# Six heads without the shift, and the first weights in quarters for four heads at once

**Chip, cores, metric.** One core of a Trainium2 chip. The metric is the device time of one execution in microseconds (us), lower is better. Executions of one kernel spread over some 5 us (0.4%).

## The reference, cut to what matters

```python
mod = silu(c) @ w_mod                      # six rows of 1024: sa, ca, ga, sb, cb, gb
h = layernorm(x) * (1 + ca) + sa           # x: 2048 x 1024
q = h @ wq                                 # 32 heads of 128
o = softmax(q k^T / sqrt(128)) v           # 4 kv heads, the last 512 keys
x = x + ga * (o @ wo)
x = x + gb * ffn(layernorm(x) * (1 + cb) + sb)
```

The change touches only the first 55 us or so. There the kernel must get x (1 MB of the first 512-row chunk), the scale columns `ca` of w_mod (2 MB), the first query weights (1 MB), the shift columns `sa` (2 MB) and keys and values from HBM before the attention can run.

## The kernel before

A helper tracks buffers and puts semaphore waits before each operation; so nearly all matmuls have the line L272. The query of a head is `(n * (1+ca) + sa) @ wq`, n the normed x. The shift `sa` comes late. So the first heads ("without the shift", NQ0 = 8) are projected from `n * (1+ca)` and kept in f32; later one column `sa @ wq` per head (16 one-column matmuls for two heads) is added: `q_bias_mm`, `q_shifted`. Other heads are projected inside the attention rounds, from shifted hT.

```python
for hf in range(2):                 # loads, in order of issue
    load_wca(hf)                    # half of the scale columns: 4 loads of 256 KB, rows of 512 columns
    load_wq0(hf)                    # half of the contraction of heads 0 to 3, 512 KB
load_wq(1)                          # heads 4 to 7, 1 MB
load_k(0)
for k2 in range(DT // 2):
    load_wsa(k2)                    # shift columns, 4 x 512 KB
load_v(0); load_wq(2); load_x(1)
# ... [cut] norm, transposes, first half of the scales; then the opening:
for kc in range(HK):
    for h in range(3):              # three heads on the first 256 rows, later on the other 256
        q_first(h, kc, 0, 2 * P)
# ... [cut] second half, head 3; then:
qproj_mm(4, ...); q_raw(4); mod_sa(0); k_turn(0, BB)     # mod_sa(k2): shift columns of load k2
qproj_mm(5, ...); q_raw(5); mod_sa(1)
qproj_mm(6, ..., 0, HK); mod_sa(2); qproj_mm(6, ..., HK, DT); q_raw(6); mod_sa(3)
qproj_mm(7, ..., 0, HK); q_bias_mm(0, 2, BB); q_shifted(0)
qproj_mm(7, ..., HK, DT); q_raw(7); q_shifted(1)
# attention, round i: scores(i-1), exp on ScalarE, pv(i-2); and in pre0(i):
if i in (1, 3, 5): q_bias_mm(i + 1, i + 3, QB)
if i < NQ0 + 1:
    if i % 2 == 0: qproj(NQ0 - 1 + i // 2)   # a projection in every second round
elif i + 3 < NDI: qproj(i + 3)
```

(`mod_sa(k2)` is 16 one-column matmuls, two rows of tiles by eight columns.)

The softmax here doesn't subtract the row's maximum and nothing guards it: scores larger than these inputs give would overflow.

## Time and profile before

| | before |
|---|---|
| median of the first 3 runs, then of 6 | 1162.29, 1159.84 us |
| lowest, highest of the 6 | 1158.30, 1163.55 us |
| span of the profiled execution | 1156.8 us, clock 1.000 |
| TensorE busy | 1145.8 us, 99% |

The prediction below shows the lines. One more view, the waits between 29.5 and 60 us (who waited for whom: us in total, times, longest), shows what the loop part of the change is after: in the first rounds TensorE's weight loads wait for exps on ScalarE, since only every second round has a projection to do.

```profile
PEld ps L272 <- ACT arena L796: 2.4, 3, 1.0
```

### The profile page before, as it was taken

How to read it: one execution, taken by the hardware profiler on the slowest of the kernel's cores; microseconds unless marked ns; L12 is line 12 of the kernel's file. 1: busy time of each engine (PE TensorE's matmuls, PEld its weight loads, DVE VectorE, ACT ScalarE, POOL GpSimd, SP SyncE). 2: the span in 40 equal slices, each digit the busy share in tenths (PEclk: the TensorE clock that was granted, in tenths of full speed). 3: DMA queues.
4: the chain of work that ended last, by engine and by line, in shares of the span. 5: the costliest groups of instructions: out<-in, count | busy, mean ns of one | idle time of the engine just before them, and what ended most of it. 6: DMA issues, size and time to landing. Idle time of an engine off the chain costs nothing.

```text
span 1156.8 us, 18111 instructions
## 1 busy us (share of the span) xinstructions
PE 1145.8 (99%) x7029; PEld 585.5 (51%) x7029; DVE 825.1 (71%) x1651; ACT 532.0 (46%) x745; POOL 67.6 (6%) x137
## 2 busy tenths in 40 slices
PE   8999999999999999999999999999999999999999
PEld 5555656654446566656444444444444444444444
DVE  4777997747667777786657898777558777776536
ACT  3867787720127777787100354454110444444110
POOL 1100231000000111111000010000000000000000
DMA  9789899986808898945764332423874423234443
GB/s 321 135 178 216 214 211 207 239 188 180 238 16 186 205 209 212 205 96 126 195 198 151 94 88 73 110 74 100 209 206 140 119 76 107 73 98 131 131 159 109
DMA packets 298532, 179.96 MB, mean 156 GB/s; under 512 B 140496, under 2 KB 287696, under 8 KB 298448
## 3 DMA queue, kind: packets, MB, share of 16 engines
q1 hardware_dynamic: 235472, 92.31, 37.3%
q10 hardware_dynamic: 54336, 55.05, 15.2%
q0 software_dynamic: 8640, 31.46, 8.6%
q8 instruction: 55, 0.90, 0.3%
q14 instruction: 29, 0.24, 0.1%
HBM read 125.96 MB, written 19.92 MB: 126 GB/s over the span
## 4 chain that ended last, share of the span: by engine, by line
PE 93%; DMA 2%; DVE 2%; issue 1%; ACT 1%; SPq 1%; DVEq 0%; ACTq 0%
PE ps L272 93%; DMA arena<-in_A_wq_dram 1%; DMA arena<-nsc 1%; DVE arena L826 1%; ACT arena L796 1%; DMA arena<-arena 1%; DVE arena L897 0%; SPq L341 0%; DVE arena L1053 0%; DVE st L417 0%; SPq L310 0%; SPq L359 0%; DVE arena L843 0%; DVE nsc L431 0%; DVE arena L1552 0%
## 5 line engine op out<-in xcount | busy, mean ns | idle before, releaser
L272 PE MATMUL ps<-arena 128*128 128x512 f16 (+2 forms) x6800 | 1140.4, 330 | 7.9 <-POOL arena L410 2.2
L272 PEld LDWEIGHTS ps<-arena 128*128 128x128 bf16 (+1 forms) x6800 | 577.8, 98 | 564.5 <-DVE arena L826 7.0
L796 ACT ACTIVATE arena<-ps 128x1024 bf16<-128x1024 f32 x256 | 261.2, 1021 | 43.7 <-PE ps L272 31.9
L829 ACT ACTIVATE tmp<-ps 128x512 f32<-128x512 f32 x167 | 99.7, 597 | 295.5 <-PE ps L272 284.6
L897 DVE TENSOR_TENSOR arena<-arena 128x512 f16<-128x512 bf16 x328 | 133.1, 418 | 3.0
L826 DVE TENSOR_TENSOR arena<-ps,tmp 128x512 bf16<-128x512 f32 (+1 forms) x134 | 91.7, 685 | 50.7 <-PE ps L272 37.8
L829 ACT ACTIVATE nsc<-ps 128x512 f32<-128x512 f32 x84 | 50.1, 596 | 93.2 <-PE ps L272 90.9
L818 DVE TENSOR_TENSOR arena<-ps,rl 128x512 f16<-128x512 f32 x128 | 88.5, 691 | 5.1 <-DVE rl L815 0.7
L826 DVE TENSOR_TENSOR arena<-ps,nsc 128x512 f16<-128x512 f32 x84 | 57.3, 686 | 41.0 <-PE ps L272 29.7
L815 DVE RECIPROCAL rl<-ps 128x4 f32<-128x4 f32 x128 | 23.0, 180 | 75.6 <-PE ps L272 74.8
L1113 DVE TENSOR_TENSOR tmp<-ps,tmp 128x512 f32<-128x512 f32 x32 | 22.0, 689 | 61.0 <-ACT tmp L829 51.4
L1537 ACT ACTIVATE arena<-arena 128x512 f16<-128x512 f16 x84 | 49.9, 624 | 32.7 <-DVE arena L826 32.7
L1037 DVE TENSOR_TENSOR arena<-arena 128x2048 f16<-128x2048 f16 (+3 forms) x56 | 56.0, 1010 | 9.3 <-PE ps L272 8.8
L829 ACT ACTIVATE arena<-ps 128x512 f32<-128x512 f32 x16 | 9.6, 597 | 90.7 <-PE ps L272 90.7
L947 DVE TENSOR_TENSOR arena<-arena 128x512 f16<-128x512 bf16 x120 | 47.8, 419 | 1.4 <-DMA arena<-in_A_wo_dram 0.4
L417 DVE BATCH_NORM_STATS2 st<-x_res 128x6 f32<-128x512 bf16 x58 | 39.5, 682 | 3.7 <-DMA x_res<-in_A_x_dram 3.4
L594 DVE SCALAR_TENSOR_TENSOR arena<-arena 128x1024 bf16<-128x1024 bf16 x32 | 38.9, 1215 | 0.0
L1552 DVE TENSOR_TENSOR arena<-arena 128x512 f16<-128x512 f16 x84 | 35.0, 416 | 0.3
L1114 DVE TENSOR_TENSOR tmp<-tmp,rowb 128x512 f32<-128x512 f32 (+1 forms) x49 | 33.6, 686 | 1.7
L431 DVE TENSOR_SCALAR nsc<-x_res,mv,rstd 128x1024 f16<-128x1024 bf16 (+1 forms) x30 | 16.2, 538 | 22.3 <-DMA arena<-nsc 21.0
L1115 DVE TENSOR_TENSOR arena<-tmp,x_res 128x512 bf16<-128x512 f32 (+1 forms) x33 | 22.3, 676 | 1.1
L826 DVE TENSOR_TENSOR arena<-ps,rowb 128x512 f16<-128x512 f32 x28 | 19.3, 689 | 3.9 <-ACT rowb L829 3.4
(85 smaller groups left out, 325.6 us busy)
## 6 DMA issues: line engine op xcount, KB each, us to landing
arena<-in_A_wq_dram SPq DMA_DIRECT2D x28, 512.0 KB, 5.1
arena<-wo_sum ACTq DMA_DIRECT2D x7, 2048.0 KB, 8.8
arena<-in_B_w_gate_dram SPq DMA_DIRECT2D x28, 512.0 KB, 4.0
arena<-in_B_w_up_dram SPq DMA_DIRECT2D x28, 512.0 KB, 5.1
arena<-wd_sum ACTq DMA_DIRECT2D x8, 1792.0 KB, 7.8
arena<-in_B_w_down_dram ACTq DMA_DIRECT2D x6, 1792.0 KB, 7.2
arena<-in_A_wo_dram POOLq DMA_DIRECT2D x16, 512.0 KB, 4.9
wo_sum<-arena POOLq DMA_DIRECT2D x16, 512.0 KB, 5.0
```

The lines of the kernel that those rows point to most:

```text
L272: T.op(PE, lambda: TE.matmul(out_ap, lhsT, rhs, start=start, stop=stop, skip_group_check=skip), reads=reads, writes=[bank_buf])
L417: T.op(DVE, lambda: V.bn_stats(st_[sl][:, hf * 6:hf * 6 + 6], x_res[:, t, hf * 512:hf * 512 + 512]), reads=[B_x[t]], writes=[B_st[sl]])
L594: T.op(DVE, lambda: V.scalar_tensor_tensor(mt[n % 2], mt[n % 2], 1.0, sc_row, op0=ALU.mult, op1=ALU.mult, accum_out=mcol[:, n:n + 1]), rea ...
L796: T.op(ACT, lambda: A.activation(ex_s[es][:, 2 * kp:2 * kp + 2, :], banks2(SCB + 2 * kp), AF.Exp, scale=att_scale), writes=[PB[SCB + 2 * k ...
L818: T.op(DVE, lambda: V.tensor_tensor(o_s[os_].rearrange("p (a b) d -> p a b d", a=2), psap(PVB * 512, [[512, 2], [130, 2], [1, P]]), rlb, A ...
L826: T.op(DVE, lambda: V.tensor_tensor(out, bank(ba), other, ADD), reads=[ob2], writes=[PB[ba], ob])
L829: T.op(ACT, lambda: A.activation(dst, bank(bk), AF.Copy), writes=[PB[bk], db])
L897: T.op(st, lambda: eng.tensor_tensor(o, a, b, op), reads=rd, writes=[wr])
L947: T.op(DVE, lambda: V.tensor_tensor(o, a, b, SUB), reads=rd, writes=[wr])
L1037: T.op(DVE, lambda: V.tensor_tensor(o, a, b, SUB), reads=rd, writes=[sb])
L1537: T.op(ACT, lambda: A.activation(o, s_, AF.Silu), reads=[sb], writes=[ob])
L1552: T.op(DVE, lambda: V.tensor_tensor(gu[blk][:, p, :], o, s_, MULT), reads=[sb, ob], writes=[B_gu[blk][p]])
```

## The change

The intent: start the first query matmuls sooner, by asking for a quarter of the scales and weights instead of half; have four heads go at once; reach the first scores sooner by projecting only six heads without the shift; give each of rounds 2 to 7 one projection, so that they are even. The order of the later loads follows: half of the second query weights before the shift columns, the other half after. Core of the diff:

```diff
-NQ0 = 8
+NQ0 = 6
-# load_wca(hf): 4 loads of 2 row blocks x 512 columns
+# load_wca(q): 8 row blocks x 256 columns, 1 load (2 for q == 0)
-for hf in range(2):
-    load_wca(hf); load_wq0(hf)
-load_wq(1); load_k(0)
-for k2 in range(DT // 2): load_wsa(k2)
-load_v(0); load_wq(2); load_x(1)
+for q in range(NQR):
+    load_wca(q); load_wq0(q)
+load_wq1(0); load_wsa(0); load_wsa(1); load_k(0); load_wsa(2); load_wsa(3)
+load_v(0); load_wq1(1); load_x(1); load_wq(2)
@@ opening [cut]
+q_four(0, 0, 2 * P)                     # 2 contraction tiles x 4 heads
+mod_ca(1); x_gain(1); x_mod(1, 0, B_hT[0])
+x_first(2, range(HK)); x_first(tl, range(HK)); x_mod(0, 2, B_h0b)
+q_four(1, 0, 2 * P); ...
+mod_ca(3); x_gain(3); x_mod(3, 0, B_hT[0]); q_four(2, 0, CH); q_four(3, 0, CH)
@@ after head 4
-qproj_mm(5), mod_sa(1), half of 6, mod_sa(2), rest of 6, mod_sa(3), half of 7, q_bias_mm, rest of 7
+mod_sa(1), half of 5, mod_sa(2), mod_sa(3), a quarter of 5, q_bias_mm, the last quarter of 5
@@ pre0(i)
-if i in (1, 3, 5): q_bias_mm(i + 1, i + 3, QB)
+if i in (1, 3): q_bias_mm(i + 1, i + 3, XB)
-if i % 2 == 0: qproj(NQ0 - 1 + i // 2)
+if 2 <= i < 8: qproj(i + 4)
```

Also in the change and not shown: three warm-up matmuls fewer (matmuls on zeros, which keep TensorE busy before its data is there), tiles 2 and 3 of x normed whole instead of in halves, other places for the transposes in PSUM, and the norms of the second chunk one round later.

More of the change, by code (lines that the diff above doesn't have):

```diff
@@ L331, in _, with load_wca @@
             HK = DT // 2
-            NQ0 = 8
+            NQ0 = 6
             ND = 12
-            B_wca = [[_Buf("wca%d_%d" % (hf, i)) for i in range(4)] for hf in range(2)]
+            NQR = DT // 2
+            B_wca = [[_Buf("wca%d_%d" % (q, i)) for i in range(2)] for q in range(NQR)]
             B_wsa = [_Buf("wsa%d" % k) for k in range(DT)]
-            wca = [arena.at(OFF_OT[2] + hf * 8 * KB, [DT, 512], BF16, B_wca[hf]) for hf in range(2)]
+            wca = [arena.at(OFF_OT[2] + q * 4 * KB, [DT, 2 * P], BF16, B_wca[q]) for q in range(NQR)]
             wsa = arena.at(OFF_OT[3], [DT, D], BF16, B_wsa)
-            def load_wca(hf):
-                for i in range(4):
-                    T.op(dq("q_wca%d_%d" % (hf, i)), lambda: SP.dma_start(
-                        wca[hf][:, 2 * i:2 * i + 2, :],
-                        w_mod[2 * i * P:(2 * i + 2) * P, D + hf * 512:D + (hf + 1) * 512].rearrange("(k p) n -> p k n", p=P)),
-                         writes=[B_wca[hf][i]])
+            def load_wca(q):
+                parts = 2 if q == 0 else 1
+                m = DT // parts
+                for i in range(parts):
+                    T.op(dq("q_wca%d_%d" % (q, i)), lambda: SP.dma_start(
+                        wca[q][:, i * m:(i + 1) * m, :],
+                        w_mod[i * m * P:(i + 1) * m * P, D + q * 2 * P:D + (q + 1) * 2 * P].rearrange("(k p) n -> p k n", p=P)),
+                         writes=[B_wca[q][i]] if parts == 2 else B_wca[q])
             NWQ = 2
@@ L356, in load_wq, with load_wq0 @@
                     wq_s[gidx], A_wq[:, gidx * 512:(gidx + 1) * 512].rearrange("(k p) n -> p k n", p=P)), writes=B_wq[gidx])
-            def load_wq0(kh):
-                T.op(dq("q_wq0%d" % kh), lambda: SP.dma_start(
-                    wq_s[0][:, kh * HK:(kh + 1) * HK, :],
-                    A_wq[kh * HK * P:(kh + 1) * HK * P, 0:512].rearrange("(k p) n -> p k n", p=P)), writes=[B_wq[0][kh]])
+            B_wq0 = [_Buf("wq0_%d" % q) for q in range(NQR)]
+            def load_wq0(q):
+                T.op(dq("q_wq0%d" % q), lambda: SP.dma_start(
+                    wq_s[0][:, 2 * q:2 * q + 2, :],
+                    A_wq[2 * q * P:(2 * q + 2) * P, 0:512].rearrange("(k p) n -> p k n", p=P)), writes=[B_wq0[q]])
             def load_wsa(k2):
@@ L395, in load_v, with load_wq1 @@
                      writes=[B_vg[gk]])
-            for hf in range(2):
-                load_wca(hf)
-                load_wq0(hf)
-            load_wq(1)
+            B_wq1 = [_Buf("wq1_%d" % m) for m in range(2)]
+            def load_wq1(m):
+                T.op(dq("q_wq1%d" % m), lambda: SP.dma_start(
+                    wq_s[1][:, :, m * 2 * P:(m + 1) * 2 * P],
+                    A_wq[:, 512 + m * 2 * P:512 + (m + 1) * 2 * P].rearrange("(k p) n -> p k n", p=P)), writes=[B_wq1[m]])
+            for q in range(NQR):
+                load_wca(q)
+                load_wq0(q)
+            load_wq1(0)
+            load_wsa(0)
+            load_wsa(1)
             load_k(0)
-            for k2 in range(DT // 2):
-                load_wsa(k2)
+            load_wsa(2)
+            load_wsa(3)
             load_v(0)
+            load_wq1(1)
+            load_x(1)
             load_wq(2)
-            load_x(1)
             for gk in range(1, Hkv):
@@ L490, in warm @@
                     mm(bank(b), zwarm[:, 0:P], zwarm, True, True, [B_zw], PB[b])
-            def x_first(t, d0=0, n=DT):
-                for dt in range(d0, d0 + n):
-                    o = (dt % 2) * CH + t * P
-                    transpose(bank_bf(dt // 2)[:, o:o + P], nsc4[t][:, dt * P:(dt + 1) * P], [B_ns4[t]], PB[dt // 2])
-            def x_gain(hf):
-                T.op(DVE, lambda: V.tensor_scalar(gain_f[:, hf * HK:(hf + 1) * HK], psap(XB * 512, [[2, HK]]), 1.0, None, op0=ALU.add),
-                     writes=[PB[XB], B_g[0]])
@@ L503, in x_mod, with x_place @@
-            def x_mod(hf, c0, n, bufs):
-                for dt in (0, 2, 1, 3):
-                    dt += hf * HK
-                    src = bank_bf(dt // 2)[:, (dt % 2) * CH + c0:(dt % 2) * CH + c0 + n]
-                    dst = hT[0][:, dt, c0:c0 + n]
-                    if dt % 4 < 2:
+            B_gq = [_Buf("gq%d" % q) for q in range(NQR)]
+            def x_place(t, dt):
+                if dt < HK:
+                    return t // 2, dt * 2 * P + t % 2 * P
+                return (0 if dt % 2 else 2), (dt - HK) // 2 * CH + t * P
@@ new lines, in x_first, with x_gain, x_mod @@
+            def x_first(t, dts):
+                for dt in dts:
+                    bk, o = x_place(t, dt)
+                    transpose(bank_bf(bk)[:, o:o + P], nsc4[t][:, dt * P:(dt + 1) * P], [B_ns4[t]], PB[bk])
+            def x_gain(q):
+                T.op(DVE, lambda: V.tensor_scalar(gain_f[:, 2 * q:2 * q + 2], psap(XB * 512, [[2, 2]]), 1.0, None, op0=ALU.add),
+                     writes=[PB[XB], B_gq[q]])
+            def x_mod(q, t, bufs):
+                n = 2 * P if q < 2 else CH
+                for dt in (2 * q, 2 * q + 1):
+                    bk, o = x_place(t, dt)
+                    src = bank_bf(bk)[:, o:o + n]
+                    dst = hT[0][:, dt, t * P:t * P + n]
+                    if (t if q < 2 else dt % 2) == 0:
@@ L509, in x_mod @@
                         T.op(DVE, lambda: V.tensor_scalar(dst, src, gain_f[:, dt:dt + 1], None, op0=ALU.mult),
-                             reads=[B_g[0]], writes=[PB[dt // 2], bufs[dt]])
+                             reads=[B_gq[q]], writes=[PB[bk], bufs[dt]])
                     else:
                         T.op(ACT, lambda: A.activation(dst, src, AF.Copy, scale=gain_f[:, dt:dt + 1]),
-                             reads=[B_g[0]], writes=[PB[dt // 2], bufs[dt]])
+                             reads=[B_gq[q]], writes=[PB[bk], bufs[dt]])
@@ L515, in _, with mod_ca @@
             MCOLS = [(j, j) for j in range(DT)]
-            def mod_ca(hf, k):
-                mod_mm(wca[hf][:, k, :], B_wca[hf][k // 2], k, MCOLS[0:HK])
+            def mod_ca(q, k0=0, k1=DT):
+                for k in range(k0, k1):
+                    mod_mm(wca[q][:, k, :], B_wca[q][k // HK], k, MCOLS[0:2])
             WB = PVB
@@ L555, in _ @@
             norm(0, 0, 0)
-            stats_only(2)
+            stats(2, 2, 0)
+            norm(1, 1, 1)
+            stats(2, 2, 1)
+            T.op(DVE, lambda: V.bn_aggr(mv[2][:, :], st_[2][:, :]), reads=[B_st[2]], writes=[B_mv[2]])
             rstd_of(2, mv[2][:, 1:2], B_mv[2], 1.0)
             rstd_of(tl, acc[:, 1:2], B_acc, 1.0 / D)
-            norm(1, 1, 1)
-            norm(2, 2, 2, 0, 512)
-            warm(12, WB)
-            x_first(0)
-            warm(3, WB)
-            for k in range(4):
-                mod_ca(0, k)
-            x_first(1)
-            for k in range(4, DT):
-                mod_ca(0, k)
-                if k == 5:
-                    warm(1, WB)
-            x_first(2, 0, HK)
-            x_gain(0)
-            x_mod(0, 0, 2 * P, B_hT[0])
-            norm_last(0, 512)
-            norm(2, 2, 2, 512, 512)
+            warm(10, WB)
+            x_first(0, range(HK))
+            warm(2, WB)
+            mod_ca(0, 0, HK)
+            warm(1, WB)
+            x_first(1, range(HK))
+            mod_ca(0, HK, DT)
+            x_gain(0)
+            x_mod(0, 0, B_hT[0])
+            x_first(0, (4, 6))
+            x_first(1, (4, 6))
+            norm(2, 2, 2)
+            norm_last(0, D)
             NL = NJ - NE
@@ L641, in qproj_mm @@
                     mm(bank(b), wq_s[sl][:, kc, hh * P:(hh + 1) * P], hT[tt][:, kc, :], kc == 0, kc == DT - 1,
-                       [B_wq[sl][kc // HK], B_hT[tt][kc]], PB[b])
+                       [B_wq[sl][kc // HK], B_hT[tt][kc]] + ([B_wq1[hh // 2]] if sl == 1 else []), PB[b])
             def qproj(i, b=QB):
@@ L653, in _ @@
             BB = SCB + 3
-            QB0 = [QB, PVB, PVB + 1, SCB, SCB + 1, SCB + 2, QB, PVB]
+            QB0 = [QB, PVB, PVB + 1, SCB + 3, SCB + 1, SCB + 2, QB, PVB]
             def q_raw(h):
@@ L696, in q_first @@
                 mm(bank(QB0[h], n, c0), wq_s[0][:, kc, h * P:(h + 1) * P], hT[0][:, kc, c0:c0 + n],
-                   kc == 0 and c0 == 0, kc == DT - 1, [B_wq[0][kc // HK], bufs[kc]], PB[QB0[h]], skip=True)
-            for kc in range(HK):
-                for h in range(3):
-                    q_first(h, kc, 0, 2 * P)
-                if kc == 2:
-                    x_first(tl, 0, HK)
-                    x_mod(0, 2 * P, 2 * P, B_h0b)
-                    norm_last(512, 512)
-            for k in range(4):
-                mod_ca(1, k)
@@ L708, in _ @@
-            x_first(2, HK, HK)
-            for kc in range(HK):
-                for h in range(3):
-                    q_first(h, kc, 2 * P, 2 * P, B_h0b)
-                if kc == 1:
-                    x_first(tl, HK, HK)
-                    for k in range(4, DT):
-                        mod_ca(1, k)
-                    x_gain(1)
-                    x_mod(1, 0, CH, B_hT[0])
-            for kc in range(HK):
-                q_first(3, kc, 0, CH)
-            for kc in range(HK, DT):
-                for h in range(4):
-                    q_first(h, kc, 0, CH)
+                   kc == 0 and c0 == 0, kc == DT - 1, [B_wq0[kc // 2], bufs[kc]], PB[QB0[h]], skip=True)
@@ new lines, in q_four @@
+            def q_four(q, c0, n, bufs=B_hT[0]):
+                for kc in (2 * q, 2 * q + 1):
+                    for h in range(4):
+                        q_first(h, kc, c0, n, bufs)
+            q_four(0, 0, 2 * P)
+            mod_ca(1)
+            x_gain(1)
+            x_mod(1, 0, B_hT[0])
+            x_first(2, range(HK))
+            x_first(tl, range(HK))
+            x_mod(0, 2, B_h0b)
+            q_four(1, 0, 2 * P)
+            x_mod(1, 2, B_h0b)
+            q_four(0, 2 * P, 2 * P, B_h0b)
@@ L723, in _ @@
+            mod_ca(2)
+            x_gain(2)
+            for t in range(2, TPC):
+                x_first(t, (4, 6))
+            for t in range(TPC):
+                x_first(t, (5, 7))
+            x_mod(2, 0, B_hT[0])
+            q_four(1, 2 * P, 2 * P, B_h0b)
+            mod_ca(3)
+            x_gain(3)
+            x_mod(3, 0, B_hT[0])
+            q_four(2, 0, CH)
+            q_four(3, 0, CH)
             for h in range(4):
                 q_raw(h)
-            T.op(DVE, lambda: V.tensor_copy(gain[0][:, :], gain_f[:, :]), writes=[B_g[0]])
+            T.op(DVE, lambda: V.tensor_copy(gain[0][:, :], gain_f[:, :]), reads=B_gq, writes=[B_g[0]])
@@ L744, in _ @@
             T.op(ACT, lambda: A.activation(kd, ks, AF.Copy), writes=[PB[BB], B_kT[0]])
-            qproj_mm(5, QB0[5], 0, DT)
-            q_raw(5)
             mod_sa(1)
-            qproj_mm(6, QB0[6], 0, HK)
+            qproj_mm(5, QB0[5], 0, HK)
             mod_sa(2)
-            qproj_mm(6, QB0[6], HK, DT)
-            q_raw(6)
             mod_sa(3)
             T.op(DVE, lambda: V.tensor_copy(mod_bf[:, 0:DT], psap(XB * 512, [[2, DT]])), writes=[PB[XB], B_mode])
-            qproj_mm(7, QB0[7], 0, HK)
+            qproj_mm(5, QB0[5], HK, HK + 2)
             q_bias_mm(0, 2, BB)
             q_shifted(0)
-            qproj_mm(7, QB0[7], HK, DT)
-            q_raw(7)
+            qproj_mm(5, QB0[5], HK + 2, DT)
+            q_raw(5)
             q_shifted(1)
@@ L1197, in wq_tick @@
             def wq_tick(sc, i):
-                d = 7 if i < NQ0 + 10 else 9
+                d = 7 if i < 18 else 9
                 hp = group_at(sc, i + d)
@@ L1236, in _ @@
             x1_tiles = ln_tiles(1)
-            NORMS = {3: (2,), 4: (0,), 5: (3, 1)}
+            NORMS = {4: (2,), 5: (0,), 6: (3, 1)}
             def pre0(i):
@@ L1245, in pre0 @@
                     scores(0)
-                if i in (1, 3, 5):
-                    q_bias_mm(i + 1, i + 3, QB)
+                if i in (1, 3):
+                    q_bias_mm(i + 1, i + 3, XB)
                 if i == 1:
@@ L1251, in pre0 @@
                 if i in (8, 9):
-                    for dt in range(6 * (i - 8), 6 if i == 8 else DT):
+                    for dt in range(DT if i == 8 else 0):
                         modulate(hT[1], B_hT[1], dt, 0, 0, B_mode, x1_tiles)
-                if i < NQ0 + 1:
-                    if i % 2 == 0:
-                        qproj(NQ0 - 1 + i // 2)
+                if i < 9:
+                    if 2 <= i < 8:
+                        qproj(i + 4)
                 elif i + 3 < NDI:
@@ L1260, in pre0 @@
                     norm_turn(1, tt, x1_tiles, (i + n) % 2)
-                if 1 <= i < 5:
+                if 2 <= i < 6:
                     next(x1_stats[1])
@@ L1276, in tick0 @@
             def tick0(i):
-                if 1 <= i < 5:
+                if 2 <= i < 6:
                     next(x1_stats[0])
```

## The prediction

> **What bounds the kernel now.** I read the page first: busy shares, then the chain that ended last.
>
> ```profile
> span 1156.8 us, 18111 instructions
> PE 1145.8 (99%) x7029; PEld 585.5 (51%) x7029; DVE 825.1 (71%) x1651; ACT 532.0 (46%) x745; POOL 67.6 (6%) x137
> PE 93%; DMA 2%; DVE 2%; issue 1%; ACT 1%; SPq 1%; DVEq 0%; ACTq 0%
> ```
>
> TensorE is the bound nearly everywhere: 93% of the last chain is matmuls. A change that adds and removes almost no matmuls can only win TensorE's idle time. So the next view is the time by stage, cut where something happens: first transposes (7.04), first query matmul (11.29), end of the first four heads (20.14), first attention scores (29.50), first query of the second token chunk (53.15). Columns are busy us (count) of PE, PEld, DVE, ACT and POOL, then the clock, DMA share and GB/s.
>
> ```profile
> 2.17:7.04 4.87, 4.87 (x16) 1.56 (x16) 3.53 (x8) 2.46 (x5) 1.12 (x4) 1.00 0.95 294
> 7.04:11.29 4.25, 3.26 (x57) 2.51 (x57) 3.04 (x8) 2.58 (x6) 2.50 (x6) 1.00 1.05 346
> 11.29:20.14 8.85, 8.58 (x89) 5.67 (x89) 3.77 (x11) 3.42 (x7) 0.00 (x0) 1.00 1.09 356
> 20.14:29.50 9.36, 9.30 (x116) 5.17 (x117) 2.64 (x8) 1.63 (x4) 0.00 (x0) 1.00 1.07 364
> 29.50:53.15 23.65, 22.20 (x225) 13.64 (x225) 19.50 (x51) 20.04 (x25) 4.06 (x10) 1.00 0.78 123
> 53.15:95.60 42.45, 42.45 (x343) 25.35 (x344) 29.19 (x60) 26.86 (x33) 4.83 (x7) 1.00 0.82 190
> ```
>
> The DMA engines are saturated (near 350 GB/s) until about 30 us, TensorE loses about 1 us in 7 to 11, a little to 29.5, 1.45 us in the first rounds of attention, and nothing in the 42 us after. What ended those waits is in the TensorE timeline (start, us, what; in brackets the idle time and its releaser):
>
> ```profile
> 11.29 1.16 PE L272 MATMUL ps<-arena 128*128 128x256 f16 x9 [0.65 <-DMA arena<-in_A_wq_dram]
> ...
> 20.14 1.90 PE L272 MATMUL ps<-arena 128*128 128x512 f16 x8 [0.27 <-DMA arena<-in_A_wq_dram]
> 21.87 0.54 PE L272 MATMUL ps<-sc_bf,arena 128*128 128x1 bf16 x16
> ...
> 31.43 3.66 PE L272 MATMUL ps<-arena 128*128 128x512 f16 x28 [0.51 <-DVE bq L668]
> ...
> 42.20 5.44 PE L272 MATMUL ps<-arena 128*128 128x512 bf16 x48 [0.38 <-ACT arena L796]
> 48.10 14.27 PE L272 MATMUL ps<-arena 128*128 128x512 bf16 x117 [0.46 <-ACT arena L796]
> ```
>
> A busy record lasts longer than the step to the next matmul (8 matmuls of 512 columns occupy 20.14 to 21.87, so 0.216 each, though one record is 0.38), so real idle is some 0.16 us more per gap than the brackets say. I therefore use steps: 0.216 us for 512 columns, half for 256, and 0.41/16 = 0.026 us for one column (21.87 to 22.28). With steps, the idle before 11.29 is 0.8, at 20.14 0.43, before 29.50 0.22, at 31.43 0.65, and four waits on exp or query copies between 35 and 53 sum to 1.6. Everything this change can reach is below 5 us of 1157: 0.4%.
>
> The last shift weights matter too. The source view of their four loads (issued 12.7 to 14.9):
>
> ```profile
> DMA to landing us min/median/max: 9.1/10.2/11.1
> ```
>
> 14.9 + 11.1 = 26.0: the last lands 0.75 before its use at 26.75. The shift is hardly hidden in the kernel before.
>
> [...] The trace shows the first warm-up matmuls slow (12 take 3.25 to 7.04, where 12 at 0.216 would be 2.6). Dropping two of these is safe[...]. [...] the order of issue sets what arrives first. The trace agrees: the two halves of the first weights, issued 4.6 and 7.8, land 11.2 and 15.8. [...] Quarters of the scale columns and halves of the second weights are rows of 256 columns, 512 bytes instead of 1 KB[...]. [...]
>
> **The change part by part.**
>
> 1. Matmuls. Heads 6 and 7 lose their bias columns: 16 x 0.026 = -0.41 us. Three or so warm-up matmuls go, but they filled a wait. 24 matmuls of 256 columns and 4 of 512 become 32 of 256: equal. Heads 6 and 7 are projected inside the attention loop instead of before it: 16 x 0.216 = 3.45 us moved, not removed.
>
> 2. Opening. Before, the first query matmul needed 1 MB x + 1 MB scale columns + 512 KB weights, landed 11.24. After, it needs 1 MB + 512 KB + 256 KB. From 7.4 (first scale chunk) to 15.76 (last half of the weights) 2816 KB landed: 338 KB/us. So 768 KB less is 2.2 us: about 9.1. The gains then go through VectorE: second tile normed about 8.0, scale quarter 8.9, two evacuations of 0.37: first query matmul about 9.5, 1.8 earlier. But only 8 matmuls of 256 (0.87) can run. The next quarter's gain queues on VectorE behind the norms of tiles 2 and 3 (their rstd on POOL ends about 10.0 and 10.8 against 9.67 and 10.6 now), to about 11.6; query matmuls resume about 12.1. What is then left: 28 x 0.216 + 32 x 0.026 + 12 x 0.056 = 7.6, so the four heads end at 19.7, the same as before (19.49 + 0.216 = 19.7). Head start 1.8 us, returned to a wait of about 1.6 in the middle. Term: 0, perhaps -1.
>
> 3. Head 4 follows. Its weights are 512 KB (heads 4 and 5) and land near 18.5 instead of 20.09: wait gone, -0.43.
>
> 4. Shift weights. Before them 512 KB less is queued: 1.45 us earlier. [...] Last landing about 25.5. TensorE has only heads 4 and half of 5, the shift matmuls and one transposition before it: 19.75 + 1.73 + 0.41 + 0.22 + 0.41 + 0.86 + 0.41 = 23.8, so it waits about 1.7 us where before it filled that with heads 6 and 7. Then 0.41, copy, 0.41 bias, copy, shifted query: scores at about 27.7 instead of 29.5. With 3.45 still to do, equal work stands at 31.15: +1.65 (part 3 included).
>
> 5. Loop. Each round is now 8 + 4 matmuls of 512 and 16 of 129 columns: 12 x 0.216 + 16 x 0.057 = 3.5 us, beside ScalarE's 2.1 (two exps of 1.02) plus 1.25 of x statistics = 3.4. Before, every second round had 1.8 of TensorE beside 3.3 of ScalarE, and those waits (0.65 and 1.6, 2.25 in all) go. New ones: projection of head 6 behind the eight shifts (0.25), round 8 without a projection (0.5), remainder 0.3. Term: -1.2.
>
> Sum: 0 + 1.65 - 1.2 - 0.4 = 0. The two doubtful terms are 2 and 4, both estimated carefully to the bad side; I take -1 us for the centre.
>
> **Rivals.** (a) The full intent: loads keep 338 KB/us whatever the packet, shift weights land 24.5, opening wait half as long: -2.5 to -3 us, 1159.5. For it: TensorE's steady work after 53 us passes any gain on. (b) DMA order takes over: wsa still lands at 26 or later[...], TensorE idles 2 us before the scores, and loop gains only pay it back: +1, 1163. For it: DMA share over 1.05 until 30 us. (c) The loop becomes bound by VectorE: per round 0.87 (reciprocal, product), 0.48, 0.69, 0.69 statistics, 0.55 norm: 3.3 against 3.5. Near, but a later norm of chunk 1 (round 6 instead of 5, eight modulations of 0.34 in round 8) could delay the second chunk's first query: +1. (d) Gains absorbed later: waits after 95 us are short and follow TensorE's own work, so I do not expect it.
>
> **Range.** Three runs of before spread 1158.3 to 1163.55, more than any of these. Centre 1162.29 - 1 = 1161.3, drawn to 1160.9 because the mean of the three is 1161.4. Range 1156.5 to 1164.5. 2% is 23 us, five times all the idle time within reach: within 2% 0.985, faster 0.005, slower 0.01 (a deadly new wait that repeats).
>
> **What would show it.** First query matmul near 9.5, a gap of over 1 us before 12; the four heads' end near 19.7; the wait at head 4 gone; a gap on w_mod before scores, which start near 27.7; ScalarE waits between 31 and 48 gone; the second chunk's first query within 1.5 us of 53.15 and the same spacing after. I am wrong if the clock drops in the opening gap, or if the last shift weights land before 24.

(Passages that rested on figures which no trace or run here shows are cut from it, among them a term of the sum: what the narrower rows of the scale columns and of the second query weights add to part 4's landing. The sum was put on record with it: 0 + 1.65 - 1.2 - 0.4 = 0, with -1 us taken for the centre. So what stands in part 4, 26.0 - 1.45 = 24.55, does not lead to the landing of 25.5; the rest is that term, the author's estimate.)

## The result, and the profile after

| | before | after |
|---|---|---|
| median of 6 runs | 1159.84 us | 1159.49 us |
| lowest, highest | 1158.30, 1163.55 | 1158.15, 1161.06 |
| ratio | | 0.9993, interval 0.9973 to 1.0013 |

Ratios here and below are the mean time of one kernel's fast runs over that of the other's of the same rounds, so not quite the ratio of the medians. From the page after: span, busy, chain. The chain no longer goes through the query weights but through w_mod.

```profile
span 1159.2 us, 17989 instructions
PE 1143.0 (99%) x6930; PEld 586.3 (51%) x7014; DVE 825.4 (71%) x1649; ACT 531.9 (46%) x744; POOL 67.1 (6%) x137
PE ps L272 94%; DMA arena<-in_w_mod_dram 1%; ACT arena L817 1%; SPq L364 1%; DVE arena L847 1%; DVE arena L918 0%; SPq L369 0%; SPq L344 0%; DVE st L432 0%; SPq L310 0%; DVE arena L864 0%; DVE arena L1573 0%; DVE arena L694 0%; DVE arena L968 0%; ACT L1558 0%
```

(Some 84 matmul records are missing from this trace: 6930 against 7014 weight loads. A missing record looks like a gap of 0.216.)

TensorE's timeline after, cut to the waits:

```profile
10.07 1.03 PE L272 MATMUL ps<-arena 128*128 128x256 f16 x8 [0.55 <-DVE arena L531]
11.49 0.55 PE L272 MATMUL ps<-sc_bf,arena 128*128 128x1 bf16 x16 [0.39 <-DMA arena<-in_w_mod_dram]
...
12.91 1.91 PE L272 MATMUL ps<-arena 128*128 128x256 f16 x16 [0.40 <-DVE arena L531]
...
17.02 5.34 PE L272 MATMUL ps<-arena 128*128 128x512 f16 x24
22.20 0.54 PE L272 MATMUL ps<-sc_bf,arena 128*128 128x1 bf16 x16
23.30 0.40 PE L276 MATMUL ps<-arena 128*128 128x128 bf16 x4 [0.55 <-DMA arena<-in_A_k_cache_dram]
...
26.12 0.55 PE L272 MATMUL ps<-sc_bf,arena 128*128 128x1 bf16 x16 [0.78 <-DMA arena<-in_w_mod_dram]
...
28.94 1.49 PE L272 MATMUL ps<-arena 128*128 128x512 bf16 x3 [0.80 <-DVE arena L694]
```

The first query matmul starts 1.2 us sooner (10.07), the wait at head 4 is gone (24 matmuls run on from 17.02), and the four heads end at 17.02 + 16 x 0.216 = 20.5. Before they ended at 19.7. Then three waits replace the two projections that were taken out: first key block, last shift columns, first shifted query. (The bracket of the last line counts a missing record; by steps that wait is some 0.6.) The last line holds a surprise: 3 matmuls of 512 columns last 1.49. Windows by stage (columns as in the prediction) show why:

```profile
17.02:22.20 5.18, 5.18 (x30) 2.35 (x28) 2.01 (x5) 1.77 (x3) 0.00 (x0) 1.00 1.07 365
22.20:28.94 6.74, 4.60 (x94) 3.09 (x94) 1.97 (x6) 1.19 (x2) 0.00 (x0) 0.92 1.10 339
28.94:34.60 5.66, 5.66 (x29) 2.35 (x29) 2.89 (x11) 2.05 (x2) 0.00 (x0) 0.50 1.37 229
34.60:55.10 20.50, 19.88 (x176) 12.04 (x177) 14.97 (x33) 16.66 (x21) 3.64 (x10) 1.00 0.56 106
```

And the same view of the same kernel, with the windows set to the edges of the clock drop:

```profile
24.48:27.89 3.41, 2.63 (x55) 1.57 (x52) 0.26 (x2) 0.00 (x0) 0.00 (x0) 1.00 1.11 339
27.89:34.71 6.82, 6.02 (x30) 2.52 (x31) 4.01 (x14) 2.64 (x3) 0.00 (x0) 0.50 1.31 248
```

The eighth value is the granted clock. From 27.89 to 34.71 it is 0.50, and each matmul of 512 columns steps 0.427 instead of 0.216. Counted by steps this costs 2.8 us. In the 3.41 us before it, 48 of TensorE's 55 records are one-column matmuls, and it waited for the last shift columns.

The ledger up to a common point, the first query matmul of the second token chunk (53.15 before, 56.45 after; from there on both run the same code): +3.3, of which 2.8 is the clock. Between there and the end the distance shrinks to 2.4 (TensorE's end 1154.0 and 1156.4), since a wait of 0.88 at 265 us is not there after.

### The profile page after: what moved, and what is told of

Read it like the earlier page. It is cut to its first block, busy times and chain, and to the rows that moved or that the text cites. A ratio compares the mean times of both kernels' runs of the same rounds, so it can differ in the third digit from the quotient of the medians.

```text
span 1159.2 us, 17989 instructions
## 1 busy us (share of the span) xinstructions
PE 1143.0 (99%) x6930; PEld 586.3 (51%) x7014; DVE 825.4 (71%) x1649; ACT 531.9 (46%) x744; POOL 67.1 (6%) x137
## 4 chain that ended last, share of the span: by engine, by line
PE 94%; DVE 2%; SPq 1%; ACT 1%; issue 1%; DMA 1%; DVEq 0%; ACTq 0%
PE ps L272 94%; DMA arena<-in_w_mod_dram 1%; ACT arena L817 1%; SPq L364 1%; DVE arena L847 1%; DVE arena L918 0%; SPq L369 0%; SPq L344 0%; DVE st L432 0%; SPq L310 0%; DVE arena L864 0%; DVE arena L1573 0%; DVE arena L694 0%; DVE arena L968 0%; ACT L1558 0%
```

## The experiments

Points are read from single matmul records and DMA landings of each profiled execution. Where the record of the first score is missing, I stepped back one matmul.

| run | four heads end | last shift columns land | first scores | second chunk's first query | TensorE ends | clock at half before 60 us |
|---|---|---|---|---|---|---|
| before | 19.7 | 25.99 | 29.50 | 53.15 | 1154.0 | no |
| before again (e7) | 20.3 | 25.93 | 29.61 | 53.26 | 1153.9 | no |
| after | 20.5 | 26.07 | 28.5 | 56.45 | 1156.4 | 6.8 us |
| after again (e8) | 20.3 | 25.39 | 27.86 | 54.42 | 1154.4 | 3.4 us |
| e1 quarters, eight heads | 20.2 | 26.39 | 29.9 | 53.54 | 1154.7 | no |
| e2 six heads only | 19.6 | 25.24 | 27.7 | 53.74 | 1155.9 | 3.4 us |
| e3 after, filled | 20.2 | 25.37 | 28.2 | 53.35 | 1154.7 | no |
| e4 wide rows | 20.2 | 24.10 | 26.8 | 51.95 | 1153.1 | no |
| e5 halves, 1 KB | 21.0 | 24.95 | 27.59 | 52.76 | 1163.1 | no |
| e6 old opening | 19.8 | 23.96 | 26.43 | 51.60 | 1153.2 | no |
| e9 old opening, filled | 20.1 | 24.00 | 26.7 | 51.86 | 1152.9 | no |
| e10 = e6 again | 19.6 | 24.11 | 26.6 | 51.74 | 1151.7 | no |

**Quarters and four heads, but eight heads without the shift.** The opening alone.

```diff
-NQ0 = 6                       # tail, rounds and later loads as in the kernel before
+NQ0 = 8
```

> The quarters and the four-heads-at-once opening of the changed kernel, but eight heads without the shift, and from head 4 on the code and load order of the kernel before. My theory: the opening alone costs about 0.8 us (its quarters land in 512-byte packets, 1.79 us per 512 KB against 1.50), so the first four heads end near 20.4 instead of 19.7; the eight heads fill the time until the shift weights land, no wait over 0.7 before the scores, the clock stays at full; the first query of the second chunk (53.15 before, 56.45 in the changed kernel) comes at 53.5 to 54.2, and time is 0 to 1 us above before. Rival 1, the quarters are where the gain is and six heads lose it: four heads end before 19 and the second chunk's first query comes before 52.3. Rival 2, only noise: within 0.3 us of before at each of these points.

Measured: median 1161.39 against 1158.91, ratio 1.0017 (1.0000 to 1.0035), clock 0.999 to 1.000. Against the first profile of before (19.7; 53.15) the four heads end 0.5 later, where my theory said 0.7, and the second chunk starts 0.4 later, at the near end of 53.5 to 54.2. Rival 1 is out. Rival 2, noise, is not: the second profile of before (20.3; 53.26) lies within 0.3 us of this run at both points. What the table does bear is that the opening gains nothing: the four heads end at 20.2 to 20.5 in the four profiles with quarters in 512-byte rows, and at 19.6 to 20.3 in the six with the old opening (means 20.3 and 19.85). TensorE's timeline shows the old waits of the rounds untouched:

```profile
31.82 3.66 PE L272 MATMUL ps<-arena 128*128 128x512 f16 x28 [0.51 <-DVE bq L686]
...
42.59 5.44 PE L272 MATMUL ps<-arena 128*128 128x512 bf16 x48 [0.38 <-ACT arena L818]
48.72 5.64 PE L272 MATMUL ps<-arena 128*128 128x512 bf16 x48 [0.69 <-ACT arena L818]
```

**Six heads, nothing else.**

```diff
 # kernel before, with:
-NQ0 = 8
+NQ0 = 6                       # and the tail and rounds of the changed kernel
```

> The kernel before with nothing but six heads without the shift instead of eight, and the attention rounds of the changed kernel; loads and opening as before. My theory: first four heads end at 19.7 as before, shift weights land at 26.0 as before, TensorE waits 1.5 us or more for them in all, scores start at 28 to 28.5, and at full clock the second chunk's first query comes at 53.2 to 53.7; with the clock halved, which I expect in some executions, 2.8 us later. Time at full clock within 0.5 us of before. Rival 1, six heads alone are the gain: second chunk's first query before 52. Rival 2, the halved clock belongs to the new opening: clock 1.000 in all executions of this kernel.

Measured: 1160.91, ratio 1.0011 (0.9996 to 1.0026); clocks 0.997 three times, 0.999 three times. So rival 2 is out: the halved clock comes with the six heads, not with the new opening. The profiled execution was at half clock for 3.4 us (about 1 us lost, by steps), so at full clock its second chunk would start near 52.7; rival 1 asked for less than 52 and is out too. Two expectations were missed: the last shift columns landed at 25.24 instead of 26.0, though the loads are those of before (25.99 and 25.93), and the scores came at 27.7 instead of 28 or later. So its 0.4 us ahead of before at the second chunk may be this early landing and not the six heads. The waits that the six heads open:

```profile
22.46 0.55 PE L272 MATMUL ps<-sc_bf,arena 128*128 128x1 bf16 x16 [0.33 <-DMA arena<-in_w_mod_dram]
...
25.29 0.55 PE L272 MATMUL ps<-sc_bf,arena 128*128 128x1 bf16 x16 [0.91 <-DMA arena<-in_w_mod_dram]
...
28.12 1.49 PE L272 MATMUL ps<-arena 128*128 128x512 bf16 x3 [0.42 <-DVE arena L673]
```

**The changed kernel, its waits filled with warm-up matmuls.**

```diff
 mod_sa(0)
+warm(3, SCB)
 k_turn(0, BB)
@@
 mod_sa(2)
+warm(4, SCB)
 mod_sa(3)
@@
 qproj_mm(5, QB0[5], HK + 2, DT)
+warm(3, SCB)
 q_raw(5)
```

(One line of buffer bookkeeping for the warm-up tile goes with it.)

> The changed kernel with ten warm-up matmuls of 512 columns (2.2 us) put where TensorE waits for the first key block (3), the last shift weights (4) and the first shifted query (3). My theory: the clock halves because the array does too little between 24.8 and 28.9, so with the fills the clock is 1.000 in every execution, the stretch from the first scores to the second chunk's first query shrinks by 2.8 us to about 25, that query comes near 53.7, and the times of all runs lie within 1 us of 1158.3. Rival 1, the halving comes from the opening or from chance: clock 0.997 still in some of the runs and a spread as before. Rival 2, the fills delay the shift matmuls themselves: scores start after 29.2.

Measured: clock 1.000 in all six executions, second chunk's first query at 53.35 instead of 56.45. The changed kernel itself had full clock (1.000) in only four of its 11 executions, and 0.997 in four. Rival 1 is out, and so is rival 2 (scores at 28.2). Two parts of my expectation were missed: the times ran from 1159.29 to 1161.37, above the 1158.3 that I expected of the quickest kernel, and the ratio was 1.0007 (0.9992 to 1.0022). Filling cures the clock, but it makes a kernel that is no better than the one before. Windows, from the first fill to the second chunk:

```profile
21.93:27.50 5.57, 5.49 (x99) 3.60 (x99) 0.93 (x3) 0.60 (x1) 0.00 (x0) 1.00 1.12 338
27.50:53.35 25.85, 25.18 (x225) 15.03 (x227) 19.62 (x48) 20.56 (x25) 3.64 (x10) 1.00 0.99 155
```

**The scale columns in rows of 1 KB.** Same bytes, same destinations, other order; the columns that arrive are the wrong ones on purpose (the check against the reference did not notice, so its tolerance is wide here).

```diff
-wca[q][:, i*m:(i+1)*m, :],  w_mod[i*m*P:(i+1)*m*P, 256 columns of quarter q]
+wca[q][:, i*m:(i+1)*m, :] as m/2 x 512,  w_mod[half as many rows, 512 columns]
```

> The changed kernel with its quarters of the scale columns loaded as half as many rows of 512 columns (1 KB) instead of rows of 256 (512 bytes), the same bytes to the same places in another order: the result is wrong on purpose. My theory: the four quarter loads take 1.5 instead of 1.79 us each, the last quarter of the first query weights lands near 16.2 instead of 17.35, the last shift weights 25 to 25.3 instead of 26.07, the four heads end 0.5 us or more earlier than 20.47, and the wait for the last shift weights halves. Rival, the total rate of the engines is the limit and not the packets: the landings stay within 0.3 us of 17.35 and 26.07.

Measured: median 1157.59, ratio 0.9984 (0.9971 to 0.9997), six times between 1156.92 and 1158.22, clock 0.999 to 1.000. Single landings: a full quarter of the scale columns takes 1.49 to 1.50 us after the load ahead of it (8.64 to 10.13, 10.89 to 12.39, 13.15 to 14.64), in the changed kernel 1.75 to 1.80 (9.65 to 11.44, 12.24 to 13.99, 14.76 to 16.56). The last first-query weights land at 15.45 instead of 17.35, the last shift columns at 24.10 instead of 26.07. The rival (total rate, not packets) is out. Of the landing's gain of 1.97, some 1.1 to 1.2 comes from four loads at 0.28; the rest is mostly that execution's own (the changed kernel again had 25.39): the second half of its first quarter landed 1.46 after the first half (7.42, 8.88), in the second profile 0.88 after it (7.82, 8.70). The four heads' end moved only 0.3 (20.2), not the 0.5 I expected, and the other runs with 512-byte quarters also end at 20.2 to 20.3: the opening hardly gets faster with its packets. VectorE's timeline shows why. The second quarter of the scales is now there at 10.13 instead of 11.44, but its gain (L521) still runs only at 11.95 (12.22 in the changed kernel), behind the norms of tiles 2 and 3, the second of which (L566) starts at 11.49, just after GpSimd's rstd for it ends (11.39). The queries resume at 12.64 instead of 12.91.

```profile
11.49 0.55 DVE L566 TENSOR_SCALAR arena<-x_res,nmean,rstd 128x1024 bf16<-128x1024 bf16 x1 [0.51 <-issue]
11.95 0.15 DVE L521 TENSOR_SCALAR gain_f<-ps 128x2 f32<-128x2 f32 x1
```

The wait for the shift columns is gone:

```profile
10.29 1.03 PE L272 MATMUL ps<-arena 128*128 128x256 f16 x8 [0.58 <-DVE arena L531]
...
23.79 0.94 PE L272 MATMUL ps<-sc_bf,arena 128*128 128x1 bf16 x32
...
27.00 0.81 PE L272 MATMUL ps<-arena 128*128 128x512 bf16 x3 [0.68 <-DVE arena L694]
```

32 one-column matmuls now run through; what is left is the chain copy, shifted query (0.68).

**Halves of the scale columns again, right results.**

```diff
-for q in range(NQR): load_wca(q); load_wq0(q)
+for hf in range(2):  load_wca(hf); load_wq0(2*hf); load_wq0(2*hf + 1)    # rows of 512 columns, 2 loads each
```

> The changed kernel with correct results and 1 KB packets: the scale columns come in halves (512 columns) again, each half ahead of two quarters of the first query weights; all else as in the changed kernel. My theory (packets of 512 bytes were the cost): last first-query weights land at 15.5 to 16 instead of 17.35, last shift weights at 24.0 to 24.6, first query matmul 0.5 to 1 us later than 10.07, the four heads still end by 20.2, the clock stays full, the second chunk's first query comes near 52, and the median is 1 to 1.5 us below before (ratio 0.9985 to 0.999). Rival, the early start that the quarters give is worth its packets: four heads end after 20.7 and the second chunk's first query after 53.

Measured: median 1159.44, ratio 1.0000 (0.9987 to 1.0014), one execution at 1167.69. The ratio, the last shift columns (24.95) and the full clock (0.997 once, 0.999 once) missed the expectation. The four heads end at 21.0 and the second chunk starts at 52.76: between my theory (20.2; 52) and the rival (over 20.7; over 53), the first number is the rival's. That the quarter start is worth something to this opening once packets are equal is not shown by this: the last first-query weights of this execution landed at 15.99, in the wide-row run at 15.45, so up to 0.5 of the 0.8 between the two can be the execution's own. The new opening is in any case not better than the old one, as the next run shows.

The execution at 1167.69 is the profiled one, and it shows how other microseconds are lost. TensorE waited 1.3 us at 146, 2.5 at 221 and 1.8 at 583. At the first two, VectorE stood still ahead of an operation that needs the next block of output-projection weights (1.48 and 3.05 us ahead of L967), and what TensorE waited for ran on VectorE only after that operation (L838 at 147.10 before TensorE's 147.85, L846 at 223.43 before its 224.17). VectorE's timeline of that execution, and its waits between 138 and 226 us there, then of the kernel before between 137 and 225:

```profile
144.14 0.89 DVE L967 TENSOR_TENSOR arena<-arena 128x512 f16<-128x512 bf16 x2 [1.48 <-DMA arena<-in_A_wo_dram]
...
222.63 0.88 DVE L967 TENSOR_TENSOR arena<-arena 128x512 f16<-128x512 bf16 x2 [3.05 <-DMA arena<-in_A_wo_dram]
```

```profile
DVE arena L967 <- DMA arena<-in_A_wo_dram: 5.9, 3, 3.0
```

```profile
DVE arena L947 <- DMA arena<-in_A_wo_dram: 0.4, 1, 0.4
```

So 5.9 us of waits for one kind of load in one execution, 0.4 in another of nearly the same code. Right after the first two of TensorE's waits its clock was at half for 3.41 us each, which by steps cost some 3.5 us more. The stretches ahead of the two halvings, and the second halved one:

```profile
146.47:149.88 3.41, 1.65 (x20) 1.08 (x19) 3.27 (x11) 3.29 (x8) 1.81 (x5) 1.00 0.68 175
221.57:224.98 3.41, 1.04 (x6) 0.41 (x5) 2.29 (x6) 0.80 (x2) 0.00 (x0) 1.00 1.20 264
224.98:228.39 3.41, 3.41 (x21) 2.19 (x19) 0.95 (x3) 2.64 (x3) 0.56 (x1) 0.50 0.82 216
```

No one-column matmul ran in the stretches ahead; TensorE stood idle there for 2.1 and 2.5 us by steps. So the half clock comes without one-column matmuls too, after gaps of 2.5 us and less. That such waits make the spread of all the kernels' times is a guess: no slow execution of the kernel before was profiled.

**The old opening, six heads, the new order of loads.**

```diff
 # e2, with the changed kernel's loads after the first query weights:
-load_wq(1); load_k(0); load_wsa(0..3); load_v(0); load_wq(2); load_x(1)
+load_wq1(0); load_wsa(0..1); load_k(0); load_wsa(2..3); load_v(0); load_wq1(1); load_x(1); load_wq(2)
```

> The opening of the kernel before (halves, three heads), with six heads without the shift and the changed kernel's order of the later loads (half of the second query weights before the shift weights, half after). My theory: the new opening gives nothing, so this is as good as the run with wide rows: four heads end at 19.7, last shift weights 24 to 24.6, the second chunk's first query 51.5 to 52.2, ratio 0.998 to 0.999; the clock halves in some executions at most. Rival, the quarters and four heads at once do help once their packets are wide: this one is 0.5 us or more later than the wide-row run (51.95) at the second chunk's first query.

Measured: second chunk at 51.60, last shift columns at 23.96, median 1158.29, ratio 1.0001 (0.9988 to 1.0013). Inside the trace my theory holds to the tenth, and the old opening beats both new ones; the rival is out. In the times the lead of 1.5 us is not to be seen. TensorE's end (1153.2) is 0.8 ahead of before, so half of the lead was lost later in that execution: waits of 0.61 at 145 and 0.67 at 574 us that the profile of before does not have.

```profile
14.86 6.86 PE L272 MATMUL ps<-arena 128*128 128x256 f16 x34
...
23.44 1.12 PE L272 MATMUL ps<-sc_bf,arena 128*128 128x1 bf16 x32
...
26.43 1.04 PE L272 MATMUL ps<-arena 128*128 128x512 bf16 x4 [0.46 <-DVE arena L683]
...
50.25 6.10 PE L272 MATMUL ps<-arena 128*128 128x512 bf16 x54 [0.46 <-ACT arena L802]
```

The last line is the wait of round 8, which has no projection; all six-head kernels have it (0.62 by steps). It is the 0.5 of the prediction's part 5.

**The kernel before against itself.**

> The kernel before against itself, for the noise: ratio 1.000 with an interval of about 0.0015 to each side, single times from 1157.5 to 1163 again, clock 1.000 in nearly all. If the ratio leaves 0.9985 to 1.0015, no difference of that size in the other runs may be read as an effect.

Measured: 1.0007 (0.9995 to 1.0020), times 1158.21 to 1162.00, clock 1.000 but for one 0.998. The noise is as expected. No ratio that is within some 0.0012 of 1, half the width of this interval, says anything by itself.

**The changed kernel again.**

> The changed kernel again. My theory: the clock is 0.997 to 0.998 in about half of the executions and those are 2 to 3 us slower than the rest; the quickest lie near 1158.2; ratio to before 0.999 to 1.001. Rival, the halved clock of the first profile was a single event: 0.999 or above in five of six.

Measured: ratio 1.0010 (0.9998 to 1.0023), times 1157.79 to 1162.06. Clock 0.997 once, 0.999 once and 1.000 three times: fewer than I said, and the rival's bound (five of six at 0.999 or above) is nearly met. Over 11 executions: the four at 0.997 have a mean of 1161.06, the other seven of 1159.00. This profile had one stretch of 3.41 us at half clock:

```profile
28.11:31.52 3.41, 3.41 (x25) 1.48 (x24) 2.54 (x11) 2.05 (x2) 0.00 (x0) 0.50 1.64 335
```

**The old opening with three fills, and once more without.**

```diff
 # e9 = e6 with
 qproj_mm(5, QB0[5], HK + 2, DT)
+warm(3, SCB)
 q_raw(5)
```

> The old opening with six heads and the new load order, plus three warm-up matmuls in its one wait of 0.6 us ahead of the first scores. My theory: the clock is 1.000 in every execution, the second chunk's first query within 0.3 of 51.60, quickest times near 1157.0; the median 0.5 to 1.5 us below before, unless later waits for the output projection's weights (which hold VectorE in some executions) take it back. Rival, the fills only delay: second chunk's first query after 52.

Measured: clock 1.000 in five of five, second chunk at 51.86, median 1157.91 against 1159.13, ratio 0.9988 (0.9971 to 1.0004), times 1157.47 to 1159.32. As expected; the quickest was not 1157.0 but 1157.5.

> The old opening with six heads and the new load order again, unfilled. My theory: second chunk's first query at 51.4 to 51.9 at full clock (1.5 us ahead of before), 0.8 to 1.5 us ahead at TensorE's end; the clock halves in one to three of six executions; ratio to before 0.998 to 1.000. Rival, the lead at 52 us is always paid back in the attention: TensorE's end within 0.3 us of 1154.0.

Measured: second chunk at 51.74, TensorE's end 1151.7, median 1158.12, ratio 0.9991 (0.9972 to 1.0010), clock 0.999 to 1.000. The rival (the lead at 52 us is always paid back) is out: this execution is 2.3 us ahead of before at the end. This opening is the best right version in the medians, with or without fills, but both intervals reach past 1.000: it is not shown to beat the kernel before in time.

## Why the prediction was right, and where a step failed

The number was right (1160.9 predicted, 1159.49 measured, range 1156.5 to 1164.5). This says little for the mechanism: the range held what rivals (a) and (b) would give (1159.5 and 1163), and was wider than the spread of the kernel before. By steps:

1. **Matmuls.** As said: 176 one-column records instead of 192.
2. **Opening: "Term: 0, perhaps -1".** Nothing was gained. First query matmul 10.07 (predicted 9.5), resumption 12.9 (12.1), four heads' end 20.2 to 20.5 (19.7); what is left after the resumption took 7.56 (7.6). Two sizes were wrong. The one that counts here is the queue on VectorE ahead of the second quarter's gain, put at 11.6: with the loads early enough (e4) the gain still ran at 11.95 and the queries resumed at 12.64, 0.5 later than predicted, as GpSimd's rstd for the last tile ended at 11.39 (10.8 predicted). The other is the row of 512 bytes: a load took 17 to 20% longer (1.75 to 1.80 against 1.50), more than the author's estimate; so the second quarter landed only at 11.44. TensorE waited for it and then for VectorE's scaling with it (0.39 and 0.40 in the timeline after), which added 0.3. (The prediction's list of stages calls 20.14 the end of the four heads; it is where head 4 starts, after its wait. Part 2 has the end, 19.7.)
3. **Head 4's wait.** Gone, but in part by luck: its weights landed at 20.16 and 18.89 in the two profiles (18.5 predicted), and the four heads ended late enough to hide the first of these. In the second profile of before, where they end at 20.3, there is no such wait either.
4. **Shift columns: +1.65.** They landed at 26.07 and 25.39 (25.5 predicted), scores at 28.5 and 27.9 (27.7). With 3.45 of projection still to do, this is +2.5 and, in the second profile, +1.8. With the old opening's loads it is (27.7 + 3.45 - 29.5) = +1.65 (e2), in an execution whose shift columns landed 0.7 early. So the term was mis-sized by 0.2 to 0.8.
5. **Loop: -1.2.** In e6, where the clock stayed full, scores to second chunk take 51.60 - 26.43 = 25.17. Minus two projections (3.45), plus 16 one-column matmuls (0.41) that before has in this stretch beyond the six-head kernel, 22.13 against 53.15 - 29.50 = 23.65: -1.5. The intent of the change works here.
6. **What failed: "Dropping two of these is safe".** The ground given for this was not shown by any trace. The conclusion drawn, that the clock would hold, was wrong, though not in the opening: it halved after 27.9 us where the six heads leave TensorE little to do, and took 1.4 (3.4 us at half) to 2.8 us (6.8 us) in the two profiles, counted by steps. The prediction had named a clock drop as what would make it wrong, but in "the opening gap". At full clock (e3) the second chunk comes at 53.35 against 53.15 before: the sum of the terms, 0, was right to 0.2. That is luck in part: there the scores (28.2) made part 4 +2.15 and not +1.65, and the loop gave -1.5 and not -1.2. The "-1" put on top of it was not earned.

Of the rivals, (b), the order of the loads taking over (its cause, the rows of 512 bytes, was put as an estimate), is nearest: those rows cost 17 to 20% (1.75 to 1.80 us against 1.50), TensorE waits some 2.2 us before the scores in the first profile (0.69, 0.92 and 0.6 by steps), and without them (e4) the second chunk starts 1.4 us earlier than in e3, both at full clock, with a median of 1157.59. But its landing at 26 or later came in one of the two profiles, and its +1 us is not shown in the times. Rival (a) had its landing (24.5) in e4 (24.10), and the lead over before at the second chunk was 1.2 there, not 2.5 to 3. Rival (d), which I did not expect, is open: some leads shrink later (e6), others grow (e10).

So what the earlier scores could have given went into packets of 512 bytes (e4), into waits that heads 6 and 7 had filled (e2), and into the half clock that these waits bring in some executions (e3). The even rounds gave 1.5 back.

## What to carry to other kernels

Work moved out of a stretch that waits for a load anyway is not a gain; it was the filling, and here also what kept TensorE's clock up (with the waits filled, e3, 1.000 in six of six executions; without, in four of 11). Cutting a load into column quarters makes its rows shorter: weigh the earlier first piece against the lower rate for all that is queued behind (here 512 KB in 1.75 to 1.80 us instead of 1.49 to 1.50). When effects are below the spread of the times, compare a fixed point of equal work inside the traces, and check the granted clock there first.

## What the traces show of the half clock and of the loads

- Half clock: in the changed kernel it came with no gap of TensorE over about 1 us before it (0.92 by steps, 0.78 by the records' ends, the longest in the 3.41 us before 27.89), in a stretch where 48 of 55 matmul records had one column. The stretches at half clock last 3.41 us (e8, 28.11 to 31.52) or 6.82 us (27.89 to 34.71). Filling 2.2 us of waits kept the clock full in six of six (e3). In e5 it halved without one-column matmuls, after gaps of 2.5 us and less.
- How much work keeps the clock full was not measured. What the stretches of 3.41 us just ahead of a halving have in common here is that few columns went through TensorE: 2608 in the changed kernel (5 matmuls of 512 and 48 of one column), 3104 in its second profile, 3111 in e2, 2048 and 3088 in e5, each matmul counted by its start. At full clock 15.8 matmuls of 512 would fit (3.41 / 0.216), some 8,100 columns. Counted in steps of 3.41 us from the halvings, both ways, no other stretch of these four traces at full clock has fewer than 3592 (start and end are left out; at the start the matmuls of 512 columns step 0.427, in the changed kernel up to 7.07). The half clock starts at 27.89, 28.11 and 26.09 in three of them. That few columns are the cause is a guess from these counts; no run varied them alone.
- Loads: 512 KB in rows of 512 bytes took 1.75 to 1.80 us, in rows of 1 KB 1.49 to 1.50: 16% less rate.
- The landing of equal loads varies between executions: the last shift columns of the changed kernel landed at 26.07 and 25.39 in two profiles, those of before and e2, with the same loads, at 25.99, 25.93 and 25.24, and one block of output-projection weights held VectorE 3.0 us in one execution.
